# Channel mixing in fp32 on one Trainium2 core: two passes over the tokens, and 2x2 blocks with seven products

## The chip, the cores and the metric

The kernel runs on one core of a Trainium2 chip. The metric is the device time of one execution in microseconds. The engines are named as in the profile: PE (TensorE, matrix multiplication), PEld (its weight loads), DVE (VectorE), ACT (ScalarE), POOL (GpSimd), SP (SyncE, which issues transfers here). SBUF is the on-chip memory, PSUM the accumulators that PE writes, DRAM the memory off the core.

## The reference

All in fp32, batch 8, 8 heads of 64 channels, 576 tokens, 512 channels, 256 token features, 1536 channel features. The four mixing weights come as float64.

```python
kv = np.einsum('bhsd,bhse->bhde', k, v)
out = np.einsum('bhsd,bhde->bhse', q, kv)
rms = np.sqrt(np.mean(out * out, axis=-1, keepdims=True) + 1e-06)
x = out / rms * g_norm                       # then (B, S, H*D) = (8, 576, 512)

h = np.maximum(x.transpose(0, 2, 1) @ w_tok1, 0.0) @ w_tok2
u = x + h.transpose(0, 2, 1)
h2 = np.maximum(u @ w_ch1, 0.0) @ w_ch2      # 512 -> 1536 -> 512 channels
return u + h2
```

## The kernel before

The batches go in four pairs (A, B). A batch has four tiles of 128 tokens and 64 tokens left over; the rests of A and B make one tile, so a pair has 9 tiles, in 3 blocks of 3 for the channel mixing.

`front` (L159) gives the attention and token mixing of a pair as a list of steps: `kv` (L164, k times v, PE line L171, then `load` of the k and v two halves on), `attend` (L203, q times kv, L206) and `attend_rem` (L210, L215) with `norm` (L181: ACT's square L185, DVE's reduction L187, small steps L188 to L199, DVE's multiplication L200 and POOL's multiplication with the gain L201, which gives x), `tok1` (L219, PE L224 and L227, ACT's relu L229), `tok2` (L231, PE L235 and L240, DVE's addition L243, which turns x into u) and `turn_u` (L245: four transposes L250 and an ACT copy L251).

`main` (L265) gives the channel mixing: for each block 12 steps `ch1` (L268: four matmuls of 384 columns, L273, and a relu by ACT L277 or DVE L279 in turn) and 9 steps `ch2` (L281: four matmuls of 512 columns, L287), with DVE's addition of u (L291) and a store.

`decode` (L100) makes fp32 of a piece of weights: POOL's product L112, DVE's clamp L114, shift L116, sign L118, exponent L120 and low word L122, POOL's addition L124. Its raw words are fetched by transfers that ACT issues, into two buffers.

The order of the work is set by `weave` (L308), which deals the steps of one list evenly among those of another; the framework then orders each engine's instructions. The first pair's front is woven with the decodes of the token weights and of `w_ch1`; the first 12 `ch1` with those of `w_ch2`; after that the front of the next pair with the channel mixing of this one:

```python
    for pair in range(B // 2):
        body = main(pair, X, U)
        fill = []
        if pair == 0:
            weave(body[:NF], [do(get_ch2, f) for f in range(NF)])
            body = body[NF:]
        if pair + 1 < B // 2:
            X, U, fill = front(pair + 1)
        weave(body, fill)
```

An fp32 matmul of the program appears in the trace as two matmul records, each with a weight load; a transpose appears as one.

Of the kernel before, what the change touches and what calls it, by code (L numbers as in the profile page):

```python
# [17 lines left out]
def kernel(  # L18
# [35 lines left out]
    NT, NB, TB = 9, 3, 3  # L54
    FG = 4
# [3 lines left out]
    consts = ctx.enter_context(tc.tile_pool(name="consts", bufs=1))  # L59
    inp = ctx.enter_context(tc.tile_pool(name="inp", bufs=2))  # L60
    qtp = ctx.enter_context(tc.tile_pool(name="qtp", bufs=3))
    xp = ctx.enter_context(tc.tile_pool(name="xp", bufs=15))
    work = ctx.enter_context(tc.tile_pool(name="work", bufs=2))
    stage = ctx.enter_context(tc.tile_pool(name="stage", bufs=2))
    mix = ctx.enter_context(tc.tile_pool(name="mix", bufs=3))
    ps_f = ctx.enter_context(tc.tile_pool(name="ps_f", bufs=4, space=bass.MemoryType.PSUM))
    ps_m = ctx.enter_context(tc.tile_pool(name="ps_m", bufs=4, space=bass.MemoryType.PSUM))
# [258 lines left out]
    def do(f, *a):  # L326
        return lambda: f(*a)
# [50 lines left out]
```

## Time and profile before

| | us |
|---|---|
| median of 3 runs | 1053.71 (1050.93 to 1053.9) |
| the profiled execution, span from its first to its last instruction | 1052.2 |
| PE busy | 1002.1 (95%) |
| PEld busy | 537.9 (51%) |
| DVE busy | 266.5 (25%) |
| ACT busy | 100.8 (10%) |
| POOL busy | 106.1 (10%) |

The profile is one execution; its time is given by its span, and the runs' median lies 1.5 us above it. Busy shares are means over stages of different kinds, so they are read by stretches; the chain that ended last goes through PE for 84% of the span, DVE for 9% and transfers for 4%.

### The profile page before, as it was taken

What the parts mean: (1) busy time and instruction counts of PE and PEld (TensorE: products, weight loads), DVE (VectorE), ACT (ScalarE), POOL (GpSimd) and SP (SyncE); (2) the same over time, 40 slices, a digit from 0 to 9 for tenths busy, and PEclk for the clock granted to TensorE, in tenths of its full rate; (3) what the DMA queues carried; (4) which work ended last, traced back from release to release, by engine and by line L of the source; (5) the groups of instructions that cost most, each with busy time, mean ns of one, the idle gap of its engine ahead of it and who ended that gap; (6) DMA issues with size and microseconds to landing.
All of it is one profiled execution on the core that took longest, in us unless ns stands there. A gap on an engine that the chain in (4) does not pass through costs nothing.

```text
span 1052.2 us, 7658 instructions
## 1 busy us (share of the span) xinstructions
PE 1002.1 (95%) x3120; PEld 537.9 (51%) x3120; DVE 266.5 (25%) x559; ACT 100.8 (10%) x214; POOL 106.1 (10%) x100
## 2 busy tenths in 40 slices
PE   4788977999999999999999999999999999999998
PEld 3643544664455466554445456554445445454553
DVE  2898773351011113330111112240011111010000
ACT  0211100020001011111001011011001000000000
POOL 1464441120000001110000000010000000000000
PEclk9789997999999999999999999999999999999999
DMA  8943342121000031300000021000000000000000
GB/s 239 323 147 116 108 142 95 66 90 55 10 11 1 20 100 46 111 10 1 10 21 1 10 65 45 11 20 1 0 21 11 10 21 0 21 10 11 21 0 30
DMA packets 33554, 53.34 MB, mean 51 GB/s; under 512 B 2416, under 2 KB 20848, under 8 KB 33520
## 3 DMA queue, kind: packets, MB, share of 16 engines
q1 hardware_dynamic: 28928, 37.76, 11.0%
q10 hardware_dynamic: 4592, 15.11, 4.6%
q8 instruction: 24, 0.39, 0.2%
q14 instruction: 10, 0.08, 0.0%
HBM read 43.42 MB, written 9.44 MB: 50 GB/s over the span
## 4 chain that ended last, share of the span: by engine, by line
PE 84%; DVE 9%; DMA 4%; POOL 2%; issue 1%; ACTq 0%; ACT 0%; POOLq 0%
PE ps_w L287 35%; PE ps_v L273 33%; PE ps_h L224 4%; PE ps_u L235 4%; PE ps_kv L171 3%; PE ps_o L206 2%; DMA raw<-in_moe_w_tok_dram 2%; DVE part L122 2%; DVE w_ch L118 1%; DVE w_ch L116 1%; DVE w_ch L114 1%; PE ps_h L227 1%; PE ps_ut L250 1%; DVE part L120 1%; POOL w_ch L124 1%; DMA raw<-in_moe_w_ch_dram 1%
## 5 line engine op out<-in xcount | busy, mean ns | idle before, releaser
L287 PE MATMUL ps_w<-w_ch,v 128*128 128x512 f32 x864 | 385.0, 598 | 10.5 <-POOL w_ch L124 10.5
L273 PE MATMUL ps_v<-uT,w_ch 128*128 128x384 f32 x1152 | 383.8, 488 | 1.1 <-DVE v L279 1.1
L273 PEld LDWEIGHTS ps_v<-uT,w_ch 128*128 128x128 f32 x1152 | 215.0, 190 | 151.7 <-issue 13.4
L287 PEld LDWEIGHTS ps_w<-w_ch,v 128*128 128x128 f32 x864 | 161.7, 191 | 208.8 <-issue 190.9
L279 DVE TENSOR_SCALAR v<-ps_v 128x384 f32<-128x384 f32 x72 | 40.0, 556 | 266.2 <-PE ps_v L273 266.2
L201 POOL TENSOR_TENSOR x<-x,g_sb 128x512 f32<-128x512 f32 x36 | 47.8, 1328 | 519.5 <-DVE x L200 517.7
L291 DVE TENSOR_TENSOR o<-ps_w,x 128x512 f32<-128x512 f32 x36 | 24.9, 692 | 259.0 <-PE ps_w L287 258.9
L171 PE MATMUL ps_kv<-v_in,k_in 128*128 128x128 f32 (+1 forms) x320 | 56.0, 323 | 14.9 <-DMA v_in<-in_v_dram 13.8
L277 ACT ACTIVATE v<-ps_v 128x384 f32<-128x384 f32 x72 | 35.3, 490 | 355.2 <-PE ps_v L273 326.4
L235 PE MATMUL ps_u<-h,w_tok 128*128 128x512 f32 x128 | 60.3, 596 | 3.4 <-DVE x L243 3.3
L171 PEld LDWEIGHTS ps_kv<-v_in,k_in 128*128 128x128 f32 (+1 forms) x320 | 48.6, 219 | 27.1 <-issue 20.8
L224 PE MATMUL ps_h<-x,w_tok 128*128 128x512 f32 x128 | 59.7, 610 | 1.7 <-DVE ms L188 1.7
L243 DVE TENSOR_TENSOR x<-ps_u,x 128x512 f32<-128x512 f32 x36 | 24.8, 689 | 96.1 <-PE ps_u L235 78.3
L206 PEld LDWEIGHTS ps_o<-kvp,qT 128*128 128x128 f32 x256 | 37.1, 214 | 16.6 <-issue 4.4
L206 PE MATMUL ps_o<-kvp,qT 128*128 128x128 f32 x256 | 38.6, 302 | 7.1 <-DVE x L200 3.7
L251 ACT COPY uT<-ps_ut 128x512 f32<-128x512 f32 x36 | 21.0, 585 | 219.3 <-PE ps_ut L250 199.8
L187 DVE TENSOR_REDUCE ms<-x 128x8 f32<-128x512 f32 x36 | 24.5, 683 | 67.5 <-ACT x L185 67.5
L224 PEld LDWEIGHTS ps_h<-x,w_tok 128*128 128x128 f32 x128 | 24.7, 195 | 32.1 <-issue 28.9
L235 PEld LDWEIGHTS ps_u<-h,w_tok 128*128 128x128 f32 x128 | 23.8, 190 | 29.8 <-issue 21.1
L124 POOL TENSOR_TENSOR w_ch<-w_ch,part 128x512 f32<-128x512 f32 x24 | 31.4, 1308 | 36.7 <-DVE part L122 34.8
L185 ACT ACTIVATE x<-ps_o 128x512 f32<-128x512 f32 x36 | 21.5, 597 | 90.1 <-PE ps_o L206 75.3
L250 PEld LDWEIGHTS ps_ut<-ident,x 128*128 128x128 f32 x144 | 17.7, 141 | 20.8 <-issue 16.9
(38 smaller groups left out, 281.1 us busy)
## 6 DMA issues: line engine op xcount, KB each, us to landing
raw<-in_moe_w_ch_dram ACTq DMA_DIRECT2D x24, 512.0 KB, 3.6
qT<-in_q_dram SPq DMA_DIRECT2D x8, 1152.0 KB, 5.6
k_in<-in_k_dram SPq DMA_DIRECT2D x16, 512.0 KB, 3.7
v_in<-in_v_dram SPq DMA_DIRECT2D x16, 512.0 KB, 5.5
out_dram<-o SPq DMA_DIRECT2D x32, 256.0 KB, 2.0
raw<-in_moe_w_tok_dram ACTq DMA_DIRECT2D x2, 576.0 KB, 6.1
raw<-in_moe_w_tok_dram ACTq DMA_DIRECT2D x2, 512.0 KB, 9.2
k_in<-in_k_dram SPq DMA_DIRECT2D x16, 64.0 KB, 3.6
```

Of the source, the lines that this page charges most:

```text
L124: nc.gpsimd.tensor_tensor(out=dst, in0=dst, in1=part, op=ALU.add)
L171: nc.tensor.matmul(ps[:, i], lhsT=k_in[r, j, ts(i, P)], rhs=v_in[r, j, ts(i, P)], start=(j == 0), stop=(j == JJ - 1))
L201: nc.gpsimd.tensor_mul(x3, x3, g_sb.to_broadcast([P, H, D]))
L206: nc.tensor.matmul(ps[:, ts(hp, P)], lhsT=qT[side][:, hp, ts(j, P)], rhs=kvp[side][:, hp], start=True, stop=True)
L224: nc.tensor.matmul(ps, lhsT=w_tok1[:, j, ts(t, P)], rhs=X[side * J + j], start=(j == 0), stop=False)
L235: nc.tensor.matmul(ps, lhsT=w_tok2[:, t, ts(i % J, P)], rhs=h1[i // J][:, t], start=(t == 0), stop=(t == NTOK - 1))
L250: nc.tensor.transpose(ps[:, c], X[i][:, ts(c, P)], ident)
L273: nc.tensor.matmul(ps, lhsT=w_ch1[:, c, ts(f, P)], rhs=U[blk][:, c], start=(c == 0), stop=(c == NC - 1))
L277: nc.scalar.activation(dst, ps, AF.Relu)
L279: nc.vector.tensor_scalar(out=dst, in0=ps, scalar1=0.0, scalar2=None, op0=ALU.max)
L287: nc.tensor.matmul(ps, lhsT=v1[i // TB, part][:, f, ts(i % TB, P)], rhs=w_ch2[:, ft], start=(ft == 0), stop=(ft == NF - 1))
L291: nc.vector.tensor_tensor(out=o, in0=ps, in1=X[i], op=ALU.add)
```

## The change

The work is split into two passes. The first does the attention and the token mixing of all four pairs and stores u to nine DRAM tensors of 512 tokens each: eight with the four full tiles of a batch, the ninth with the four tiles of left-over tokens. The second fetches a group of 512 tokens, transposes it and does the channel mixing, one group after the other. The decodes of the channel weights (eight of 768 columns for `w_ch1`, twelve of 512 for `w_ch2`) are dealt among the steps of the first pass.

Both channel products are made as 2x2 blocks: the channels in two halves, the tokens (or outputs) in two halves. Seven products of blocks are made, of sums of blocks on either side, in place of eight. The sums of weights are made once (`mix_ch1`, `mix_ch2`, on POOL), those of the transposed tokens per group (`mix_u`, on DVE), those of the intermediate per round (on DVE and POOL), and the results are put together from PSUM by DVE. A bank of PSUM takes a second product on top of one whose value has been read before.

Smaller edits: `decode` has its first step on ACT and its clamp on POOL; `norm` works on two tiles at a time; k and v have their half tile padded with zeros; the two sides' half-tile matmuls take turns.

```diff
-        nc.gpsimd.tensor_scalar(out=dst, in0=hi.bitcast(F32), scalar1=2.0 ** -112, scalar2=1.0,
-                                op0=ALU.mult, op1=ALU.mult)
-        nc.vector.tensor_scalar(out=dst, in0=dst, scalar1=TOP, scalar2=-TOP,
-                                op0=ALU.min, op1=ALU.max)
+        nc.scalar.activation(dst, hi.bitcast(F32), AF.Copy, scale=2.0 ** -112)
+        nc.gpsimd.tensor_scalar(out=dst, in0=dst, scalar1=TOP, scalar2=-TOP,
+                                op0=ALU.min, op1=ALU.max)
...
+    def mix_ch1():
+        w = [w_ch1[:, i] for i in range(7)]
+        combine(w[4], w[6], w[3], ALU.add)
+        combine(w[5], w[4], w[0], ALU.subtract)
+        combine(w[6], w[0], w[6], ALU.subtract)
+        combine(w[2], w[1], w[5], ALU.subtract)
...
+            if i == 8:
+                nc.sync.dma_start(u_dram[B][ts(pair, P)], x)
+            elif i % 2 == 1:
+                nc.sync.dma_start(
+                    u_dram[2 * pair + i // J][ds((i % J - 1) * P, 2 * P)]
+                    .rearrange("(t p) e -> p t e", p=P), X[pair, i // 2])
...
+    def mix_u(g):
...
+        sub(t1, b[0, 1], b[0, 0])
+        sub(t2, b[1, 1], t1)
+        sub(b[0, 1], b[1, 1], b[0, 1])
+        sub(t4, b[1, 0], t2)
...
+    def channel1(g, d):
...
+        def product(n, ps, start, stop):
+            for w in range(W):
+                for c in range(2):
+                    nc.tensor.matmul(ps[:, w], lhsT=w_ch1[:, n - 1, c, ts(W * d + w, P)],
+                                     rhs=uc[g][n - 1][:, c], start=(start and w == 0 and c == 0),
+                                     stop=stop, skip_group_check=True)
...
+        product(1, p1, True, False)
+        nc.scalar.copy(t1, p1)
+        product(6, p6, True, True)
+        add(u2, p6, t1)
+        product(7, p7, True, False)
+        add(u3, p7, u2)
+        product(5, p5, True, False)
+        add(a22, p5, u3)
+        nc.scalar.activation(a22, a22, AF.Relu)
+        product(2, p1, False, True)
+        nc.scalar.activation(a11, p1, AF.Relu)
+        product(4, p7, False, True)
+        add(a12, p7, u2)
+        nc.scalar.activation(a12, a12, AF.Relu)
+        product(3, p5, False, True)
+        add(s3, p5, u2)
+        nc.vector.scalar_tensor_tensor(out=s1, in0=s3, scalar=0.0, in1=a22,
+                                       op0=ALU.max, op1=ALU.add)
+        nc.vector.scalar_tensor_tensor(out=s3, in0=s3, scalar=0.0, in1=a11,
+                                       op0=ALU.max, op1=ALU.subtract)
+        nc.gpsimd.tensor_tensor(out=s2, in0=s1, in1=a11, op=ALU.subtract)
+        nc.gpsimd.tensor_tensor(out=s4, in0=a12, in1=s2, op=ALU.subtract)
...
+    def channel2(g):
+        def product(n, ps, start, stop):
+            for p in range(2):
+                for s in range(NS):
+                    nc.tensor.matmul(ps[:, p], lhsT=V[g, s // 2][n - 1][:, s % 2, ts(p, P)],
+                                     rhs=w_ch2[:, n - 1, s], start=(start and p == 0 and s == 0),
+                                     stop=stop, skip_group_check=True)
...
+        return [first, sixth, seventh, fifth, second, fourth, third]
...
+    weave(attention(0), weights)
+    weights = [do(get_ch1, i, c) for i in range(2) for c in range(NC)] + [mix_ch1]
+    weights += [do(get_ch2, f) for f in range(NF)] + [mix_ch2]
+    steps = []
+    for pair in range(B // 2 - 1):
+        weave([do(steps.append, f) for f in token_mixing(pair)],
+              [do(steps.append, f) for f in attention(pair + 1)])
+    weave(steps, weights)
...
+    late["m"] = pool("m", 6, space=bass.MemoryType.PSUM)
...
+    for g in range(NG):
+        fetch_u(g + 1)
+        for d in range(NS // 2):
+            channel1(g, d)
+        weave(channel2(g), prepare(g + 1, t_psum))
```

In the diff, `combine` is one POOL addition or subtraction of 1536 columns, `sub` and `add` are one DVE instruction each (`add` reads PSUM), W is 2, NS is 6, and the weights woven with `attention(0)` are the token weights. The functions left out of the diff do what their like did before. In the new program k times v is line L216, attention L251 and L260, the gain multiplication L244, the norm's multiplication L243, the token products L279, L283, L292 and L297, the addition of u L301, the transposes L324, the first channel product L365, the second L404.

How the instructions stand on an engine is shown at three places. On PE, at the end of the first pair's front and the start of its channel mixing before (ps_v and ps_w are the two channel products, ps_ut the transposes, xN is a count of equal matmuls):

```order
L235 MATMUL ps_u<-h_452,w_tok_87 128x512 x2
L250 MATMUL ps_ut<-ident,x 128x128 x4
L240 MATMUL ps_u<-h_427,w_tok_87 64x512 x2
L240 MATMUL ps_u<-h_452,w_tok_87 64x512 x2
L250 MATMUL ps_ut<-ident,x 128x128 x12
L273 MATMUL ps_v<-uT,w_ch_88 128x384 x48
L287 MATMUL ps_w<-w_ch_89,v_662 128x512 x4
L287 MATMUL ps_w<-w_ch_89,v_727 128x512 x4
L171 MATMUL ps_kv<-v_in,k_in 128x128 x10
```

and now, from the last transposes of the second group through its first products (ps_w_1645 takes the last product of the group before, the others are the four banks of a round):

```order
L324 MATMUL ps_ut<-ident,xg 128x128 x4
L404 MATMUL ps_w_1645<-w_ch_89,vs_0_1483 128x256 x2
L404 MATMUL ps_w_1645<-w_ch_89,vs_1_1538 128x256 x2
L404 MATMUL ps_w_1645<-w_ch_89,vs_2_1593 128x256 x2
...
L365 MATMUL ps_v_1786<-uT,w_ch_88 128x256 x4
L365 MATMUL ps_v_1787<-t_1771,w_ch_88 128x256 x4
L365 MATMUL ps_v_1788<-uT,w_ch_88 128x256 x4
L365 MATMUL ps_v_1789<-t_1770,w_ch_88 128x256 x4
L365 MATMUL ps_v_1786<-uT,w_ch_88 128x256 x4
L365 MATMUL ps_v_1788<-t_1772,w_ch_88 128x256 x4
L365 MATMUL ps_v_1789<-uT,w_ch_88 128x256 x4
```

Where runs of 48 and of 4 matmuls of 384 and 512 columns stood, with the next pair's k times v between them, there are now products of 4 (and of 12) matmuls of 256 columns that take turns among PSUM banks, and nothing of the attention. On DVE at the same turn of groups now (there was none before; ps_w_1644 and ps_w_1645 hold the second channel product's last two results, L330 is `mix_u`, L369 and L389 the sums of a round):

```order
L408 TENSOR_TENSOR xg<-ps_w_1644,xg 128x2x256
L330 TENSOR_TENSOR t_1770<-uT 128x512
L330 TENSOR_TENSOR t_1771<-uT,t_1770 128x512
L330 TENSOR_TENSOR uT<-uT 128x2x256
L330 TENSOR_TENSOR t_1772<-uT,t_1771 128x512
L408 TENSOR_TENSOR xg<-ps_w_1645,xg 128x2x256
L369 TENSOR_TENSOR u_1791<-ps_v_1787,t_1790 128x512
```

The four differences of the next group's tokens stand ahead of the last addition of this one. On POOL in the decode of the channel weights before (L201 is the gain multiplication, w_ch_88 is `w_ch1`), the stretch after the first pair's last x:

```order
L201 TENSOR_TENSOR x<-x,g_sb 128x512
L124 TENSOR_TENSOR w_ch_88<-w_ch_88,part 128x512 x2
L112 TENSOR_SCALAR w_ch_88<-raw 128x512 x2
L124 TENSOR_TENSOR w_ch_88<-w_ch_88,part 128x512 x2
L112 TENSOR_SCALAR w_ch_88<-raw 128x512 x2
L124 TENSOR_TENSOR w_ch_88<-w_ch_88,part 128x512
```

and now, from the first pair's last x (the first row) to two of the second pair (w_ch_89 is `w_ch2`, L185 a sum of weights):

```order
L244 TENSOR_TENSOR x<-x,g_sb 128x1024
L134 TENSOR_SCALAR w_ch_88<-w_ch_88 128x768 x2
L144 TENSOR_TENSOR w_ch_88<-w_ch_88,part 128x768 x2
...
L134 TENSOR_SCALAR w_ch_88<-w_ch_88 128x768
L134 TENSOR_SCALAR w_ch_89<-w_ch_89 128x2x256
L244 TENSOR_TENSOR x<-x,g_sb 128x1024
L144 TENSOR_TENSOR w_ch_88<-w_ch_88,part 128x768
L185 TENSOR_TENSOR w_ch_88<-w_ch_88 128x1536 x4
L244 TENSOR_TENSOR x<-x,g_sb 128x1024
L144 TENSOR_TENSOR w_ch_89<-w_ch_89,part 128x2x256
```

The gain multiplications of the second pair, which before came after all decodes, now stand between them and the sums of weights.

## Rows read from the trace of the kernel before

**Rows 1.** The page's slices: busy tenths of PE, and GB/s of the transfers, 40 slices.

```profile
PE   4788977999999999999999999999999999999998
...
GB/s 239 323 147 116 108 142 95 66 90 55 10 11 1 20 100 46 111 10 1 10 21 1 10 65 45 11 20 1 0 21 11 10 21 0 21 10 11 21 0 30
```

**Rows 2.** Windows: stretch, its length, busy us (count) per engine, clock, transfers.

```profile
174.30:861.97 687.67, 687.67 (x2182) 365.85 (x2182) 126.96 (x301) 70.05 (x151) 34.19 (x27) 1.00 0.09 31
861.97:1047.70 185.73, 185.73 (x506) 95.57 (x504) 16.02 (x27) 9.41 (x19) 0.00 (x0) 1.00 0.04 13
```

**Rows 3.** PE in order of time: start, length, line, tile, columns, count.

```profile
861.97 31.13 PE L273 MATMUL ps_v<-uT,w_ch 128*128 128x384 f32 x96
892.93 31.06 PE L287 MATMUL ps_w<-w_ch,v 128*128 128x512 f32 x72
923.83 31.12 PE L273 MATMUL ps_v<-uT,w_ch 128*128 128x384 f32 x96
```

**Rows 4.** Groups of the page: busy us, mean ns of one, idle before and its releaser.

```profile
L273 PEld LDWEIGHTS ps_v<-uT,w_ch 128*128 128x128 f32 x1152 | 215.0, 190 | 151.7 <-issue 13.4
...
L251 ACT COPY uT<-ps_ut 128x512 f32<-128x512 f32 x36 | 21.0, 585 | 219.3 <-PE ps_ut L250 199.8
```

**Rows 5.** PE in order of time, records of 128 columns.

```profile
181.25 1.05 PE L206 MATMUL ps_o<-kvp,qT 128*128 128x128 f32 x8
182.14 3.60 PE L287 MATMUL ps_w<-w_ch,v 128*128 128x512 f32 x8
...
193.34 2.97 PE L171 MATMUL ps_kv<-v_in,k_in 128*128 128x128 f32 x20
196.24 3.70 PE L287 MATMUL ps_w<-w_ch,v 128*128 128x512 f32 x8
```

**Rows 6.** DVE in order of time, from the first pair's last x on.

```profile
68.47 0.68 DVE L200 TENSOR_TENSOR x<-ps_o,inv 128x512 f32<-128x512 f32 x1
...
80.11 1.37 DVE L116 TENSOR_SCALAR w_ch<-w_ch 128x512 uint32<-128x512 uint32 x1
...
85.39 0.43 DVE L114 TENSOR_SCALAR w_ch<-w_ch 128x512 f32<-128x512 f32 x1 [1.99 <-POOL w_ch L112]
85.85 0.43 DVE L116 TENSOR_SCALAR w_ch<-w_ch 128x512 uint32<-128x512 uint32 x1
86.31 0.69 DVE L118 SCALAR_TENSOR_TENSOR w_ch<-raw,w_ch 128x512 uint32<-128x512 uint32 x1
87.03 0.43 DVE L120 TENSOR_SCALAR part<-w_ch 128x512 uint32<-128x512 uint32 x1
87.38 0.68 DVE L243 TENSOR_TENSOR x<-ps_u,x 128x512 f32<-128x512 f32 x1
87.98 0.68 DVE L122 SCALAR_TENSOR_TENSOR part<-raw,part 128x512 f32<-128x512 uint32 x1
...
108.39 0.68 DVE L243 TENSOR_TENSOR x<-ps_u,x 128x512 f32<-128x512 f32 x1
```

**Rows 7.** POOL in order of time, decodes of the channel weights.

```profile
74.55 1.27 POOL L124 TENSOR_TENSOR w_ch<-w_ch,part 128x512 f32<-128x512 f32 x1 [2.28 <-DVE part L122]
...
79.83 1.37 POOL L124 TENSOR_TENSOR w_ch<-w_ch,part 128x512 f32<-128x512 f32 x1 [1.09 <-DVE part L122]
...
92.65 0.65 POOL L112 TENSOR_SCALAR w_ch<-raw 128x512 f32<-128x512 f32 x1 [2.52 <-DMA raw<-in_moe_w_ch_dram]
...
111.88 1.27 POOL L124 TENSOR_TENSOR w_ch<-w_ch,part 128x512 f32<-128x512 f32 x1 [2.28 <-DVE part L122]
```

**Rows 8.** Transfers by line: count, KB each, median us from issue to landing.

```profile
qT<-in_q_dram SPq DMA_DIRECT2D x8, 1152.0 KB, 5.6
```

**Rows 9.** ACT in order of time: its issues of the token weights' transfers.

```profile
22.76 7.61 ACTq L145 DMA_DIRECT2D raw<-in_moe_w_tok_dram  x2
```

**Rows 10.** All engines in order of time, the end of the span.

```profile
1047.75 0.69 DVE L291 TENSOR_TENSOR o<-ps_w,x 128x512 f32<-128x512 f32 x1 [9.61 <-PE ps_w L287]
1048.47 1.11 SPq L299 DMA_DIRECT2D out_dram<-o  x2
```

More of the change, by code (lines that the diff above doesn't have):

```diff
@@ L64, with pool @@
[L64 to L67, printed above, removed]
+    def pool(name, bufs, side="left", stack=ctx, **kw):
+        return stack.enter_context(tc.tile_pool(name=name, bufs=bufs, side=side,
+                                                reuse_waits="tile", **kw))
@@ new lines @@
+    consts = pool("consts", 1)
+    dram = ctx.enter_context(tc.tile_pool(name="dram", bufs=1, space=bass.MemoryType.DRAM))
+    right = ExitStack()
+    xp = pool("xp", 9, "right", right)
+    hp_ = pool("hp", 2, "right", right)
+    left = ExitStack()
+    inp = pool("inp", 1, "left", left)
+    qtp = pool("qtp", 2, "left", left)
+    stage = pool("stage", 2, "left", left)
+    work = pool("work", 2, "left", left)
+    psums = ExitStack()
+    ps_o = pool("ps_o", 2, "left", psums, space=bass.MemoryType.PSUM)
@@ L86, in load, with do, w_psum @@
+    def do(f, *a):
+        return lambda: f(*a)
+    def w_psum(shape, name):
+        return ps_w.tile(shape, F32, name=name, tag="w")
+    qT = {}
     def load(n):
@@ new lines, in norm, with attend @@
+            nc.gpsimd.tensor_mul(x3, x3, g_sb.to_broadcast([P, n * H, D]))
+        def attend(c):
+            side = c // 2
+            ps = ps_o.tile([P, 2, DM], F32, name="ps_o", tag="o")
+            for t in range(2):
+                for hp in range(HP):
+                    nc.tensor.matmul(ps[:, t, ts(hp, P)],
+                                     lhsT=qT[2 * pair + side][:, hp, ts(2 * (c % 2) + t, P)],
+                                     rhs=kvp[side][:, hp], start=True, stop=True)
+            norm(ps, c, 2)
@@ new lines, in attend_rem @@
+        def attend_rem():
+            ps = ps_o.tile([P, 1, DM], F32, name="ps_o", tag="o")
+            for hp in range(HP):
+                for side in range(2):
+                    nc.tensor.matmul(ps[ds(side * HF, HF), 0, ts(hp, P)],
+                                     lhsT=qT[2 * pair + side][:, hp, LO:],
+                                     rhs=kvp[side][:, hp], start=True, stop=True)
+            norm(ps, 4, 1)
+        return [do(kv, 0, 0), do(kv, 0, 1), do(attend, 0), do(kv, 1, 0), do(attend, 1),
+                do(kv, 1, 1), do(attend_rem), do(attend, 2), do(attend, 3)]
@@ L212, in attend_rem, with token_mixing, tok1 @@
+    def token_mixing(pair):
+        h1 = {}
+        def tok1(t):
+            ps = []
+            for side in range(2):
+                if t == 0:
+                    h1[side] = hp_.tile([P, NTOK, DM], F32, name="h1")
+                ps.append(w_psum([P, DM], "ps_h"))
+                for j in range(J):
+                    nc.tensor.matmul(ps[side], lhsT=w_tok1[:, j, ts(t, P)],
+                                     rhs=x_of(pair, side * J + j), start=(j == 0), stop=False)
             for side in range(2):
@@ new lines, in tok2 @@
+            x = x_of(pair, i)
+            nc.vector.tensor_tensor(out=x, in0=ps, in1=x, op=ALU.add)
+            if i == 8:
[4 more added lines that the diff above has]
+                    .rearrange("(t p) e -> p t e", p=P), X[pair, i // 2])
+        return [do(tok1, t) for t in range(NTOK)] + [do(tok2, i) for i in range(9)]
+    xg, uT, uc = {}, {}, {}
```

276 lines of the change are left out of this document (140 added, 136 removed).

## The prediction

> **What bounds the kernel now.** I read the page's slices first, then the stretches by windows, then TensorE's order of time, and last the decode of the weights on VectorE (DVE) and GpSimd (POOL). In the slices TensorE (PE) is below 9 tenths busy only in the first seven [rows 1]. From 174.30 to 1047.70 us it never idles, at a granted clock of 1.00, which is the 2.4 GHz level [rows 2]. So there are two regimes: a start of 174 us in which PE waits for others, and 873 us that are nothing but PE's instructions. A change pays in the second only by taking PE time away, and in the first only by shortening what PE waits for.
>
> The price of a PE instruction is exact in the second regime. Each fp32 matmul of the program is two matmul records. The 96 records of 384 columns of one block run from 861.97 to 892.93, so 30.96/96 = 322.5 ns each, and the 72 of 512 columns that follow run 30.90/72 = 429.2 ns each [rows 3]. The difference is 106.7 ns for 128 columns; what is left beside 0.833 ns a column is 2.5 ns a record. The weight load before each record lasts 190 ns [rows 4] and is hidden at both sizes. At 128 columns eight records of the attention product take 0.89 us (181.25 to 182.14), 111 ns each, but the 20 of k times v 2.90 us (193.34 to 196.24), 145 ns each [rows 5].
>
> **The channel products.** Before: twelve such blocks, 1152 records of 384 and 864 of 512 columns, 371.5 + 370.8 = 742.3 us. After, a group of 512 tokens has three rounds of 7 products with 4 matmuls, and then 7 products with 12: 168 matmuls, all of 256 columns. Nine groups are 1512 matmuls, 3024 records. No row has 256 columns. The line through 384 and 512 gives 322.5 - 106.7 = 215.8 ns; halfway between 111 and 322.5 is 217. From below nothing beats the columns alone, 213 ns; from above the surplus of the k-times-v records over the other 128-column ones (145 - 111 = 34) may be a cost of changing weights quickly, which would make 250. I take 215.8, since two long rows and the eight fast records lie on one line: 3024 x 215.8 = 652.6 us. **That takes away 89.7 us**, by 7/8 of the columns in half as many records again.
>
> The Trainium skill, "TensorE: Matmul & The Clock Gate", section "Back-to-back issue gap", speaks against this change: in a stream of pairs of weight load and matmul both set the spacing, some 81 ns at N=128 where the columns alone give 56. With that surplus of 25 ns the products would take 728 us and all but 14 us of the gain would be gone; the 111 ns rows stand against it, the 145 ns rows for it.
>
> **The sums between products.** In each round DVE adds five products from PSUM (0.68 us each, by the like addition L243) and makes two sums in SBUF (0.69, by the like decode step L118): 4.8 us [rows 6]. ACT makes four passes of about 0.6 [rows 4], POOL two sums of 1.27 [rows 7]. A round is 56 records, 12.1 us of PE, so all of it lies beside PE. The order lets it: a bank that is read after product 1, 7 or 5 is written again two or three products later (1.7 us each), and the four banks of a round rotate over six. Where the second channel product begins, PE has 5.2 us of product 1 and four more matmuls before it needs POOL's last sum, which comes 0.68 + 0.69 + 1.27 = 2.6 us after its input. Where the next group begins, the four differences (4 x 0.7 = 2.8 us) stand on DVE ahead of the last addition, beside the 5.2 us of the last product. I cost these at nothing; if that cover failed, each 0.1 us per product would be 252 x 0.1 = 25 us. The group's read from DRAM is asked for a whole group (74 us) ahead, against 5.6 us for a read of like size [rows 8]. Transposes stay 16 a group: 8 groups x 16 x 0.111 = 14.2 us in this pass.
>
> **The first pass.** It loses its cover. Before, attention and token mixing of pairs 1 to 3 ran between channel matmuls, and what they waited for cost nothing. Now the first pass has only its own PE work: k times v and attention 320 records each at 111, token products 320 at 429, and the first group's transposes: 35.5 + 35.5 + 137.3 + 1.8 = 210 us, 52 a pair. (The padded half tile of k and v removes the 64-row records.)
>
> Beside it stands the decode. In the old trace DVE takes 0.43 + 0.43 + 0.69 + 0.43 + 0.68 = 2.66 us for 512 columns (85.39 to 87.98, five steps [rows 6]) and POOL 0.65 + 1.27 = 1.92, and between POOL's additions of 74.55 and 111.88 lie eight decodes, 4.67 us each: the sum of both and not the longer one [rows 7]. DVE's rows show why: its shift (L116) takes 0.43 us alone, but 1.37 where it starts behind a POOL addition of 1.37, while an addition from PSUM beside a POOL step takes its usual 0.68 [rows 6, 7]. So I add DVE's decode steps to POOL's work, and let its PSUM operations and reductions lie beside POOL.
>
> The Trainium skill, "GPSIMD Engine Reference", section "Key points", draws the same line: POOL shares its SBUF interfaces with DVE instructions in a two-port mode or with two SBUF inputs.
>
> The change gives ACT the first step and POOL the clamp: a decode of 512 is then 2.23 + 1.92 = 4.15, one of 768 is 6.2, and the eight sums of 1536 weights are 3.8 us of POOL each (1.27 per 512). Per pair, POOL's gain multiplication is 9 x 1.27 = 11.4 and DVE's small steps in SBUF some 3.5.
> - To the last x of pair 0: before at 69.2 us [rows 6] with three channel decodes behind it. Now the same three are larger (3 x 1.6) and the five token decodes cheaper (5 x 0.4): 72 us.
> - To the last x of pair 1: five decodes of 768, four of 512, four weight sums, attention: 31 + 16.6 + 15.3 + 14.9 = 78, so 150. PE has 52 there and waits.
> - To the last x of pair 2: eight decodes, four sums, attention: 33.2 + 15.3 + 14.9 = 63, so 213.
> - Then POOL's last multiplication and the rest of the first token product (24 records and the half tiles): 2.5 + 11.5, so 227. From there PE bounds: one pair's 52, then the last second token product and the transposes, 17.2 + 1.8: **pass one ends at 298 us**.
>
> Bounds: if DVE and POOL did not collide, DVE alone has 56 us in the second stage, PE leads from there, and the pass ends near 258. If all of DVE's work added up with POOL's (20 us more in the second stage, 13 in the third), near 331. I take 298 because eight decodes in a row ran at the sum. The intermediate's 9.4 MB out and 9.4 MB back are little beside the 323 GB/s of the second slice [rows 1]. On SP a store of it waits for DVE's addition and holds the k and v loads behind it; they have two buffers and are needed some 9 us later.
>
> **The end.** Before, the last addition starts at 1047.75 and the span ends 4.4 us later, with two stores at 0.55 us of issue each [rows 10]. Now there are four: 5.5 us. I give 2 us to the change of pools between the passes.
>
> **The sum.** 298 + 2 + 652.6 + 14.2 + 5.5 = 972.3 us of span, against 1052.2 now. The shown runs' median, 1053.7, lies 1.5 above that span, so **974 us**, 7.6% less. The products save 89.7; the first pass gives some 10 of it back.
>
> **The rivals.**
> 1. *The first pass is bound by PE, not by DVE and POOL* (it ends at 258): 934 us. For it: POOL also waited up to 2.52 us for its raw data [rows 7], so the 4.67 may hold latency that attention can fill. Against: nine additions were filled in between 87.38 and 108.39 already [rows 6], and the pace stayed.
> 2. *The first pass stretches* (it ends at 331): 1007 us. Everything on DVE and POOL adds up, or the weight DMAs that ACT issues, each waiting for a free raw buffer, hold up ACT's squares and roots. For it: two such issues kept ACT for 7.61 us [rows 9].
> 3. *Weight loads show at 256 columns*, the slower case: 215.8 + 34 = 250 ns a record, 103 us more, 1077 us. It decides from (1053.7 - 974)/3024 = 26.4 ns a record on. For it: the 145 ns records, and a weight load of 190 ns before a record of 213. Against: the eight records at 111, with a load before each; and 4 of the 20 slow ones are 64 rows high, a better reason for their surplus. The page on TensorE named above gives this mechanism 25 ns a record, 1050 us.
> 4. *The change doesn't do what it says*, its columns not falling to 7/8: the order of its instructions, 1512 matmuls of 256 columns, rules it out.
>
> **How the numbers follow.** My forecast 62%, rival 1 15%, rival 2 17%, rival 3 6%. The range from 935 to 1012 holds the forecast, its bounds and nearly all of rivals 1 and 2. Some 0.3% is what a measurement can tell from no change. Rival 3 alone gives slower (5%) or, at three quarters of its price, no change (1%); the rest, 94%, is faster.
>
> **What would show it.** Right: L365 and L404 with 1512 records each, 215 to 217 ns apart; DVE and ACT waiting for PE there, and PE for nothing; a boundary between the passes near 298 us; PE idle between 72 and 227 us, released by the gain multiplication (L244) or DVE's multiplication (L243). Wrong: gaps of PE before products with a releaser on DVE, ACT or POOL; records more than 225 ns apart; a granted clock below 1.00 in the second pass; a boundary before 270 or after 325 us.

## The result, and the profile after

The changed kernel takes 978.3 us (median of four runs) beside 1053.8 for the kernel before in the same comparison: a ratio of 0.930 with a 95% interval from 0.927 to 0.933. The forecast was 974, with a range from 935 to 1012. The profiled execution has a span of 975.2 us.

| | before | after |
|---|---|---|
| span of the profiled execution, us | 1052.2 | 975.2 |
| PE busy, us | 1002.1 | 896.6 |
| PEld busy, us | 537.9 | 723.8 |
| DVE / ACT / POOL busy, us | 266.5 / 100.8 / 106.1 | 383.1 / 148.5 / 246.2 |

The page's slices of the changed kernel, PE's busy tenths and its granted clock (40 slices of 24.4 us), which answer to [rows 1]:

```profile
PE   3749669769999999999999999999999999999997
...
PEclk9879879889999999999999999999999999999999
```

PE is below nine tenths in seven of the first nine slices, then in none but the last. The windows of the stages (stretch, length, then busy us and count of PE, PEld, DVE, ACT and POOL, clock, share and GB/s of the transfers); the cuts are the ends of the four first token products, the first channel product and PE's last record:

```profile
12.12:84.51 72.39, 47.51 (x200) 31.50 (x200) 50.83 (x77) 15.28 (x25) 34.92 (x24) 0.83 0.76 238
84.51:159.70 75.19, 57.61 (x242) 33.57 (x241) 60.12 (x84) 15.87 (x28) 44.84 (x27) 0.86 0.56 186
159.70:231.95 72.25, 55.81 (x243) 33.68 (x241) 49.39 (x73) 12.23 (x23) 37.19 (x21) 0.91 0.52 167
231.95:302.23 70.28, 68.68 (x299) 38.09 (x297) 30.95 (x60) 12.52 (x24) 10.68 (x5) 1.00 0.39 135
302.23:969.20 666.97, 666.97 (x3154) 586.97 (x3152) 189.04 (x276) 89.96 (x149) 115.70 (x81) 1.00 0.07 25
969.20:975.20 6.00, 0.03 (x1) 0.00 (x0) 0.69 (x1) 0.00 (x0) 0.00 (x0) 0.95 0.38 89
```

Two regimes again. From 302.23 to 969.20 us PE is busy for all of 666.97 us; before that, it waits for 73 of 302. PE in order of time, at the start of the first second channel product (the answer to [rows 3]):

```profile
338.59 5.34 PE L404 MATMUL ps_w<-w_ch,v 128*128 128x256 f32 x24
343.77 5.34 PE L404 MATMUL ps_w<-w_ch,vs 128*128 128x256 f32 x24
348.95 0.60 PE L324 MATMUL ps_ut<-ident,xg 128*128 128x128 f32 x4
```

24 records take 5.18 us twice, 215.8 ns each. The groups of the second pass (busy us, mean ns; idle before) show what waits there:

```profile
L365 PE MATMUL ps_v<-uT,w_ch 128*128 128x256 f32 x864 | 201.3, 379 | 0.0
...
L365 PEld LDWEIGHTS ps_v<-uT,w_ch 128*128 128x128 f32 x864 | 164.1, 190 | 23.1 <-issue 0.8
```

PE waits for nothing there, and the weight load of 190 ns is hidden beside a record of 215.8. (The 379 ns are a record's own length, with a modelled end; what counts is the distance from one start to the next.) In the first pass DVE and POOL, in order of time, behind pair 1's first x (in brackets the idle time before and its releaser):

```profile
112.08 14.18 POOL L185 TENSOR_TENSOR w_ch<-w_ch 128x1536 f32<-128x1536 f32 x4
```

```profile
86.95 0.56 DVE L136 TENSOR_SCALAR w_ch<-w_ch 128x768 uint32<-128x768 uint32 x1 [6.40 <-POOL w_ch L134]
...
104.16 0.16 DVE L240 SCALAR_TENSOR_TENSOR root<-root,ms 128x16 f32<-128x16 f32 x1
...
112.21 1.21 DVE L230 TENSOR_REDUCE ms<-x 128x16 f32<-128x1024 f32 x1
113.34 0.68 DVE L301 TENSOR_TENSOR x<-ps_u,x 128x512 f32<-128x512 f32 x1
...
116.39 3.11 DVE L238 SCALAR_TENSOR_TENSOR ms<-ms,inv 128x16 f32<-128x16 f32 x1
...
119.63 3.27 DVE L240 SCALAR_TENSOR_TENSOR root<-root,ms 128x16 f32<-128x16 f32 x1
```

Four sums of weights hold POOL for 14.18 us, 3.5 each. While they run, a reduction and an addition from PSUM take their usual 1.21 and 0.68 us. Two steps of 16 columns, whose like takes 0.16 at 104.16, take 3.11 and 3.27, until 119.50 and 122.90, just behind the ends of the second and the third sum (112.08 + 2 x 3.55 and + 3 x 3.55). But at 86.95 DVE has idled for 6.40 us with the decode on its way. The waits of the same pass (total us, times, longest) say what for; below them ACT in order of time, ahead of that step.

```profile
DVE w_ch L136 <- POOL w_ch L134: 31.2, 11, 6.4
ACT w_ch L133 <- DMA raw<-in_moe_w_ch_dram: 30.2, 11, 6.3
```

```profile
84.61 0.60 ACT L286 ACTIVATE h<-ps_h 128x512 f32<-128x512 f32 x1 [6.66 <-PE ps_h L283]
85.11 0.90 ACT L133 ACTIVATE w_ch<-raw 128x768 f32<-128x768 f32 x1
```

So two things stretch the first pass: the collision of POOL's long instructions with DVE's (theory A, the forecast's), and a round trip of the decode, raw transfer to ACT to POOL to DVE, with two raw buffers (theory B). The longest wait, at 86.95, is neither alone: ACT has the decode's first step (L133) behind a relu that waited 6.66 us for PE. No run moves that step alone. The experiments separate theories A and B as far as they can, and test the second pass.

### The profile page after: what moved, and what is told of

Read it like the earlier page. It is cut to its first block, busy times and chain, and to the rows that moved or that the text cites. A ratio compares the mean times of both kernels' runs of the same rounds, so it can differ in the third digit from the quotient of the medians.

```text
span 975.2 us, 10020 instructions
## 1 busy us (share of the span) xinstructions
PE 896.6 (92%) x4128; PEld 723.8 (74%) x4128; DVE 383.1 (39%) x573; ACT 148.5 (15%) x252; POOL 246.2 (25%) x169
## 4 chain that ended last, share of the span: by engine, by line
PE 78%; DVE 11%; DMA 4%; POOL 4%; issue 1%; ACT 1%; SPq 0%; ACTq 0%; DVEq 0%; POOLq 0%
PE ps_v L365 33%; PE ps_w L404 33%; PE ps_u L292 3%; DMA raw<-in_moe_w_ch_dram 3%; PE ps_h L279 3%; PE ps_kv L216 2%; DVE part L142 2%; PE ps_ut L324 2%; POOL w_ch L185 1%; POOL x L244 1%; DVE x L243 1%; PE ps_o L251 1%; DVE w_ch L138 1%; DVE part L140 1%; DVE ms L230 1%
## 5 line engine op out<-in xcount | busy, mean ns | idle before, releaser
L365 PE MATMUL ps_v<-uT,w_ch 128*128 128x256 f32 x864 | 201.3, 379 | 0.0
L404 PE MATMUL ps_w<-w_ch,vs 128*128 128x256 f32 x864 | 192.1, 379 | 0.0
L365 PEld LDWEIGHTS ps_v<-uT,w_ch 128*128 128x128 f32 x864 | 164.1, 190 | 23.1 <-issue 0.8
L404 PEld LDWEIGHTS ps_w<-w_ch,vs 128*128 128x128 f32 x864 | 162.3, 190 | 21.1
L393 POOL TENSOR_TENSOR vs<-vs,v 128x512 f32<-128x512 f32 x27 | 47.6, 1764 | 428.3 <-DVE vs L389 410.4
L365 PE MATMUL ps_v<-t,w_ch 128*128 128x256 f32 x648 | 153.1, 379 | 0.0
L404 PE MATMUL ps_w<-w_ch,v 128*128 128x256 f32 x648 | 144.1, 379 | 0.0
L365 PEld LDWEIGHTS ps_v<-t,w_ch 128*128 128x128 f32 x648 | 123.1, 190 | 16.7
L404 PEld LDWEIGHTS ps_w<-w_ch,v 128*128 128x128 f32 x648 | 122.5, 190 | 16.3
L279 PE MATMUL ps_h<-x,w_tok 128*128 128x512 f32 x128 | 65.5, 654 | 16.4 <-POOL x L244 16.4
L369 DVE TENSOR_TENSOR v<-ps_v,u 128x512 f32<-128x512 f32 x54 | 37.3, 692 | 102.1 <-PE ps_v L365 102.1
L251 PE MATMUL ps_o<-kvp,qT 128*128 128x128 f32 x256 | 40.2, 319 | 30.4 <-DVE x L243 17.7
L251 PEld LDWEIGHTS ps_o<-kvp,qT 128*128 128x128 f32 x256 | 37.7, 228 | 40.5 <-issue 23.0
L279 PEld LDWEIGHTS ps_h<-x,w_tok 128*128 128x128 f32 x128 | 25.0, 208 | 52.9 <-issue 29.0
L292 PE MATMUL ps_u<-h,w_tok 128*128 128x512 f32 x128 | 61.8, 614 | 1.4 <-ACT h L286 1.4
L244 POOL TENSOR_TENSOR x<-x,g_sb 128x1024 f32<-128x1024 f32 (+1 forms) x20 | 44.2, 2210 | 61.4 <-DVE x L243 58.6
L216 PEld LDWEIGHTS ps_kv<-v_in,k_in 128*128 128x128 f32 x320 | 41.0, 206 | 20.8 <-issue 19.5
L216 PE MATMUL ps_kv<-v_in,k_in 128*128 128x128 f32 x320 | 42.1, 291 | 13.9 <-DMA v_in<-in_v_dram 13.9
```

The source lines that it names most:

```text
L216: nc.tensor.matmul(ps[:, i], lhsT=kk[:, j, ts(i, P)], rhs=vv[:, j, ts(i, P)], start=(j == 0), stop=(j == JJ - 1))
L244: nc.gpsimd.tensor_mul(x3, x3, g_sb.to_broadcast([P, n * H, D]))
L251: nc.tensor.matmul(ps[:, t, ts(hp, P)], lhsT=qT[2 * pair + side][:, hp, ts(2 * (c % 2) + t, P)], rhs=kvp[side][:, hp], start=True, stop=True)
L279: nc.tensor.matmul(ps[side], lhsT=w_tok1[:, j, ts(t, P)], rhs=x_of(pair, side * J + j), start=(j == 0), stop=False)
L292: nc.tensor.matmul(ps, lhsT=w_tok2[:, t, ts(i % J, P)], rhs=h1[i // J][:, t], start=(t == 0), stop=(t == NTOK - 1))
L365: nc.tensor.matmul(ps[:, w], lhsT=w_ch1[:, n - 1, c, ts(W * d + w, P)], rhs=uc[g][n - 1][:, c], start=(start and w == 0 and c == 0), stop= ...
```

## The experiments

All times are medians; ratios are to the kernel before, measured beside it. The stages, read from the one profiled execution of each kernel: the end of the first token product of pairs 0 to 3 and the start of the first channel product, us.

| kernel | time | ratio, 95% interval | pair 0 | pair 1 | pair 2 | pair 3 | second pass |
|---|---|---|---|---|---|---|---|
| the change | 978.3 | 0.927 to 0.933 | 84.6 | 159.8 | 232.0 | 284.7 | 302.2 |
| e1_eight | 1053.7 | 0.9996 to 1.0022 | 85.5 | 152.4 | 215.1 | 267.9 | 286.3 |
| e2_no_wsum | 964.8 | 0.914 to 0.918 | 89.8 | 156.7 | 220.8 | 273.5 | 291.0 |
| e3_raw5 | 970.4 | 0.919 to 0.924 | 90.9 | 164.2 | 225.0 | 277.8 | 295.3 |
| e4_dve | 959.8 | 0.909 to 0.913 | 82.0 | 149.2 | 214.9 | 267.7 | 285.2 |
| s1_sums_twice | 982.0 | 0.929 to 0.934 | 86.7 | 161.6 | 236.4 | 289.1 | 306.6 |
| f2_late_dve | 949.5 | 0.899 to 0.902 | 82.0 | 143.3 | 203.6 | 256.4 | 273.9 |
| f3_late_dec | 972.6 | 0.921 to 0.926 | 86.2 | 152.1 | 204.8 | 256.8 | 290.1 |
| f4_late_dec_dve | 957.1 | 0.905 to 0.910 | 81.0 | 143.1 | 195.9 | 247.8 | 280.0 |
| g1_late_raw5 | 953.1 | 0.903 to 0.906 | 85.3 | 146.2 | 206.9 | 259.7 | 277.3 |
| g2_late_sp | 961.3 | 0.911 to 0.914 | 81.7 | 143.6 | 196.4 | 249.1 | 282.0 |
| h1_spread | 940.6 | 0.891 to 0.895 | 82.5 | 133.7 | 190.1 | 244.2 | 261.9 |

**The two passes alone.**

```diff
+    def channel1(g, f):
+        v = V[g, f] = late["v"].tile([P, DM], F32, name=f"v{f}")
+        ps = m_psum([P, DM], "ps_v")
+        for c in range(NC):
+            nc.tensor.matmul(ps, lhsT=w_ch1[:, c, ts(f, P)], rhs=uT[g][:, c],
+                             start=(c == 0), stop=(c == NC - 1))
...
+        def tile_of(t):
+            ps = m_psum([P, DM], "ps_w")
+            for f in range(NF):
+                nc.tensor.matmul(ps, lhsT=V[g, f][:, ts(t, P)], rhs=w_ch2[:, f],
+                                 start=(f == 0), stop=(f == NF - 1))
```

> The two passes alone: the second pass makes eight products of 512 columns in place of seven of 256, and no sums of weights, tokens or results are made. The second pass has 9 x 192 x 2 = 3456 records of 429.2 ns, some less at its transposes: 742 from the first to the last product's records of 512 x 2 x 864 (1728 matmuls, 3456 records at 214.6 ns per 256 columns) + 14 = 756 us against the 667 measured with the scheme. The first pass also loses its eight sums of weights. If POOL's and DVE's work add up in the first pass (theory A), it ends near 275 instead of 302 and the span is about 275 + 756 + 6 = 1037 us. If the decode's round trip and its raw buffers set the pace (theory B), the sums lie beside waiting, the pass ends near 295 and the span is about 1057. Either way the scheme is worth about 90 us in the second pass; if the sums or weight loads had cost PE anything there, it would be less.

It takes what the kernel before takes, within the 0.3% that can be told. Its first pass ends at 286.3, halfway between theory A's 275 and theory B's 295. Its window of the second pass, beside the change's 666.97 (PE's 1856 records are 1728 of 512 columns and 128 transposes; the 3456 of the expectation count 256 columns each):

```profile
286.26:1046.63 760.37, 758.02 (x1856) 341.27 (x1856) 61.59 (x89) 51.07 (x86) 0.00 (x0) 1.00 0.06 21
```

So the scheme takes 93.4 us from the second pass, and the first pass is 15.9 longer with it (302.2 against 286.3); the tail is 1.3 longer. The net, 76.2, is the 76.1 between the spans (1051.3 and 975.2). Dividing the work into passes, with the smaller edits, gains nothing and costs nothing by itself.

**The sums of weights left out.**

```diff
-    weights += [do(get_ch2, f) for f in range(NF)] + [mix_ch2]
+    weights += [do(get_ch2, f) for f in range(NF)]
```

(`mix_ch1` likewise. DVE fills the empty slots with zeros at the start of the kernel, from 2.53 to 11.57 us.)

> The sums of weights are left out (their slots hold zeros, so three of seven products of each kind are wrong; PE's work is the same). Eight POOL instructions of 3.5 us go. Theory A (POOL's work and DVE's decode steps add up): pass one ends near 275 us, the time is about 951. Theory B (round trip of the decode, raw buffers): at most 8 us less, about 970. The second pass stays at 667 us.

11.2 us less in the first pass: neither 27 nor 8 at most. The second and third stage are 67 and 64 us in place of 75 and 72. Each lost 14 us of POOL and gave back 8. The first stage is 5.2 us longer, with the zeros ahead of the decode on DVE; without that the sums are worth some 16 us, like the 15.9 of e1_eight, which has none either, and half of the 30.6 that the forecast charged. Either POOL's work and DVE's do not add up in full, or another wait takes the place of the sums; this run does not tell which. Nor do the busy times of the windows, since DVE's 60.12 us in the second stage hold the time in which it stood behind POOL.

**Five raw buffers.**

```diff
     def fetch(n):
+        i = turn[0] = (turn[0] + 1) % 5
+        if i < 3:
+            spare = w_ch2[:, 3 + i].rearrange("p s n -> p (s n)").bitcast(U32)
+            return spare[:, :2 * n].rearrange("p (n w) -> p n w", w=2)
         return stage.tile([P, n, 2], U32, name="raw", tag="raw")
```

> Five raw buffers instead of two, three of them in slots of w_ch2 that are not written before its sums. Theory A: no change within 5 us (978). Theory B: the stops behind raw transfers go; four of them in the chain of waits between 91 and 190 us last 7.07, 6.02, 4.28 and 5.79 us, 23 together, so the time falls to about 955. If the issues from ACT stood in ACT's way, they no longer wait for a buffer, and that gain is in the same number.

The third stage falls from 72.3 to 60.8 us, the second from 75.2 to 73.3, and the first grows by 6.3, since more channel decodes come ahead of the first pair's x: eight of the large ones are done by its end in place of five. The stages' gains are thus in part work moved forward, and the net is what counts: 6.9 us of the first pass, 7.9 of the median. Theory B is real, and a third of the 23 us that it forecast.

**All of the decode's POOL work on DVE.**

```diff
-        nc.gpsimd.tensor_scalar(out=dst, in0=dst, scalar1=TOP, scalar2=-TOP,
+        nc.vector.tensor_scalar(out=dst, in0=dst, scalar1=TOP, scalar2=-TOP,
...
-        nc.gpsimd.tensor_tensor(out=dst, in0=dst, in1=part, op=ALU.add)
+        nc.vector.tensor_tensor(out=dst, in0=dst, in1=part, op=ALU.add)
...
-        nc.gpsimd.tensor_tensor(out=o, in0=a, in1=b, op=op)
+        nc.vector.tensor_tensor(out=o, in0=a, in1=b, op=op)
```

> The clamp, the last addition and the sums of weights move from POOL to DVE; POOL keeps the gain multiplication alone. Theory A: the collisions go. DVE has about 24 units of 512 columns x 3.34 = 80 us of channel decode, 17 of token decode, 16 of weight sums and 20 a pair of its own, 193 us in all by 227, so PE leads more often: pass one ends at 260 to 270 and the time is about 940. Theory B: the round trip loses two crossings between engines but waits for raw data as before: 5 to 10 us less, about 970. Rival: DVE becomes the bound itself and the first pass is longer than 302 us.

17 us gained in the first pass, more than from five buffers or from leaving the sums out, though DVE was given all that work. 959.8 lies between theory A's 940 and theory B's 970 and decides for neither. DVE is then near to being the bound: it is busy for 58.3 of 67.2 us in the second stage and 54.9 of 65.7 in the third. The window from 120 to 160 us:

```profile
120.00:160.00 40.00, 29.34 (x110) 15.45 (x109) 35.62 (x60) 7.60 (x14) 8.05 (x3) 0.91 0.46 149
```

Here DVE (the third pair of numbers) is busy for 35.62 of 40 us and PE (the first) for 29.34.

**DVE's additions in the second pass made twice.**

```diff
+            nc.vector.tensor_tensor(out=tmp(shape, "spare"), in0=ps, in1=x, op=ALU.add)
             nc.vector.tensor_tensor(out=o, in0=ps, in1=x, op=ALU.add)
```

> In the second pass each of DVE's additions from PSUM is made twice, the first time into a spare tile: 9 groups x (3 x 5 + 6) = 189 more of about 0.65 us, 123 us of DVE in 667, and every sum is ready 0.65 us later than before. If the sums lie beside the products with room, as I costed them, the time stays at 978 within 3 us: DVE goes from about 28% to 46% of the second pass and the results of a product are wanted only after the next one (1.73 us). Rival: the chain of sums stands at the edge already; then 0.65 us for each of the 189 shows in part, 30 to 120 us more.

```profile
306.56:973.50 666.94, 666.94 (x3154) 587.37 (x3152) 303.69 (x464) 86.90 (x149) 115.98 (x81) 1.00 0.07 25
```

The second pass is the same to 0.03 us with DVE at 303.69 us instead of 189.04, so the 3.7 us more in the whole come from the first pass (306.6 against 302.2). Every engine has the same instructions in the same order there; some 4 us is thus what the first pass of one order of work can differ by between two kernels, and nothing is built on less below.

**The sums behind pair 3's last x, and the decode on DVE.**

```diff
+            last[:] = [square, nc.vector.tensor_mul(x3, o, inv.to_broadcast([P, n * H, D])),
+                       nc.gpsimd.tensor_mul(x3, x3, g_sb.to_broadcast([P, n * H, D]))]
...
+            with tc.issue_after(last[0].ins), tc.issue_after(last[1].ins), tc.issue_after(last[2].ins):
+                f(*a)
...
-    weave(token_mixing(3), prepare(0, lambda: w_psum([P, NC, P], "ps_ut")))
+    weave(token_mixing(3), mix_ch1() + mix_ch2() + prepare(0, lambda: w_psum([P, NC, P], "ps_ut")))
```

(`issue_after` keeps an engine's order; `mix_ch1` and `mix_ch2` now return lists of single sums, each of them run through the middle lines.)

> The eight sums of weights stay on POOL but are queued behind pair 3's last gain multiplication, where POOL was busy for 11 of 70 us; the decode's clamp and last addition move to DVE, so that POOL has the gain multiplication alone beside DVE's decode. Theory A (what POOL and DVE do in SBUF adds up): the run with everything on DVE ended its first pass at 285 us with DVE busy for some nine tenths of the time up to 200 us; 14 us of weight sums leave DVE, so 272 us, time about 946. Theory B (raw transfers set the pace): no more than 4 us off that run, about 956.

949.5: 3 us from theory A, 7 from B. With the 4 us above this favours A and does not settle it. POOL's sums cost nothing where DVE has little but additions from PSUM: from pair 3's first token product to the second pass it is 17.5 us with them and without.

**Eight late decodes as well.**

```diff
-    weights += [do(get_ch2, f) for f in range(NF)] + [mix_ch2]
+    weights += [do(get_ch2, f) for f in range(4)]
...
+    weave(token_mixing(3), mix_ch1() + [behind(get_ch2, f) for f in range(4, NF)] + mix_ch2() +
+          prepare(0, lambda: w_psum([P, NC, P], "ps_ut")))
```

> Engines of the decode as in the changed kernel. The eight sums of weights and the decodes of the last eight of twelve pieces of w_ch2, raw transfers included, are queued behind pair 3's last x, under the 70 us in which PE is busy throughout; stages two and three keep eight decodes of 768 columns and four of 512. Theory A: 16 units of 4.15 instead of 24, and no sums: 33 + 15 = 48 us for either stage, less than PE's 52, so each stage takes 55 to 58 us instead of 75 and 72, and the pass ends near 270: about 945. Theory B: the first eight pieces come at the same pace as before, and the second stage stays near 66 us as without sums; the third falls to 55: the pass ends near 278, about 953. Danger: the late decodes take 63 us beside PE's 70, and the first products wait for them.

> Both together: late sums on POOL, eight late decodes, clamp and last addition of every decode on DVE. Theory A: DVE has 16 x 3.34 = 53 us of decode in stages two and three together and about 20 a stage of its own, 47 a stage, under PE's 52: the pass ends near 265, about 940; as good as or a little better than with the decode's engines unchanged. Theory B: the same as that run within 4 us.

972.6 and 957.1 miss both theories of either kernel. The third stage falls to PE's own 52.8 us in both, as forecast. The last stage gives it back: 33 and 32 us from pair 3's first token product to the second pass instead of 17.5. The second of the two kernels in order of time, first POOL, then DVE, ACT and PE:

```profile
238.24 14.31 POOL L185 TENSOR_TENSOR w_ch<-w_ch 128x1536 f32<-128x1536 f32 x4
```

```profile
242.07 7.21 DVE L136 TENSOR_SCALAR w_ch<-w_ch 128x512 uint32<-128x512 uint32 x2
249.20 4.50 DVE L138 SCALAR_TENSOR_TENSOR w_ch<-raw,w_ch 128x512 uint32<-128x512 uint32 x2
```

```profile
255.05 0.33 ACTq L180 DMA_DIRECT2D raw<-in_moe_w_ch_dram  x1
255.43 0.60 ACT L290 ACTIVATE h<-ps_h 128x512 f32<-128x512 f32 x1 [15.75 <-issue]
```

```profile
261.77 12.92 PE L296 MATMUL ps_u<-h,w_tok 128*128 128x512 f32 x26 [12.92 <-ACT h L290]
```

PE's wait points at ACT's relu, the relu stands behind an issue of a raw transfer, and the issue waited for a raw buffer which DVE held through two steps of 3.6 us that take 0.43 alone. Which link matters, the issue on ACT or the collision, the next run decides.

**ACT taken out of the late decodes; five buffers with the decode on DVE.**

```diff
-        nc.scalar.dma_start(raw, words(moe_w_ch2)[ts(f, P)])
+        (nc.sync if late else nc.scalar).dma_start(raw, words(moe_w_ch2)[ts(f, P)])
...
+        if late:
+            nc.gpsimd.tensor_scalar(out=dst, in0=hi.bitcast(F32), scalar1=2.0 ** -112,
+                                    scalar2=1.0, op0=ALU.mult, op1=ALU.mult)
```

> The run with late sums, eight late decodes and the decode on DVE, in which PE stood still for 12.92 us before the second token product of pair 3: ACT had an issue of a raw transfer ahead of its relu, and that issue waited for a raw buffer. Here the eight late pieces are fetched by SP and their first step is POOL's; ACT has nothing of them. If the issue on ACT is the cause, the 12.9 us go and the time is about 944. If the collision of POOL's sums of weights with DVE's decode is the cause, PE waits for DVE (the addition of u) instead and the time stays near 957.

PE's wait stays, at 12.0 us, now for DVE's addition of u (L311), which stands behind the decode steps. POOL (L190 is a sum of weights), DVE and PE in order of time:

```profile
242.76 10.56 POOL L190 TENSOR_TENSOR w_ch<-w_ch 128x1536 f32<-128x1536 f32 x3
```

```profile
242.84 3.64 DVE L139 TENSOR_SCALAR w_ch<-w_ch 128x512 f32<-128x512 f32 x1 [6.52 <-POOL w_ch L135]
246.51 3.53 DVE L141 TENSOR_SCALAR w_ch<-w_ch 128x512 uint32<-128x512 uint32 x1
250.08 3.79 DVE L143 SCALAR_TENSOR_TENSOR w_ch<-raw,w_ch 128x512 uint32<-128x512 uint32 x1
```

```profile
268.16 7.51 PE L302 MATMUL ps_u<-h,w_tok 128*128 128x512 f32 x12 [11.96 <-DVE x L311]
```

So the issue on ACT is not the cause; it only passed the wait on. Each of the three steps lasts as long as one sum of weights, 3.5 us, instead of 0.43 or 0.69: that is 9.4 us, and 6.52 more go by before them, while POOL has the decode's first step between two sums. What is not parted here is how long PE would wait for an addition of u behind late decodes that collide with nothing. 961.3 is 4 us worse than with ACT, which is not read as a difference.

> The run with late sums and the decode on DVE, and beside it five raw buffers instead of two (three in slots of w_ch2 that its sums write later). If waits for raw data still cost what five buffers gave back when POOL and DVE both decoded (8 us), the time falls from 949.5 to about 942. If they only show beside collisions, it stays at 949.5 within 2 us: DVE, busy for some nine tenths of the second and third stage, is then what bounds them.

No gain; the 3.6 us more are the first stage's 3.3. The second and third stage are 60.9 and 60.7 us against 61.3 and 60.3, so raw buffers no longer hold them. That DVE does is not shown: in f2_late_dve it is busy for 52.8 and 47.0 us of these two stages, less than the nine tenths that I had put down, and PE for 54.0 and 53.4.

**All on DVE, dealt by stage.**

```diff
+    weights[7:] = [behind(1, weights[7])] + [behind(1, get_ch2, f) for f in range(6)]
...
+    weave(token_mixing(3), mix_ch1() + [behind(3, get_ch2, f, True) for f in range(6, NF)] +
+          mix_ch2() + prepare(0, lambda: w_psum([P, NC, P], "ps_ut")))
```

(With the edits of e4_dve and g2_late_sp; `behind(p, ...)` queues behind pair p's last x.)

> All of the decode and the sums of weights on DVE, so that POOL has nothing with two SBUF inputs but the gain multiplication, and the work dealt by stage: seven pieces of w_ch1 up to pair 1's last x, the eighth and six of w_ch2 behind it, the other six pieces (fetched by SP, first step on POOL) and the eight sums behind pair 3's last x. If the collision of POOL's long additions with DVE was what made the late decodes cost what they gave, DVE has about 25 + 25 us a stage in stages two and three (under PE's 52) and 58 of the last 70: stages of 55 to 58, 53 and 53 us, pass one ends at 262 to 268, the time is about 938. If it is the late decodes as such (DVE's additions of u queued behind them), PE waits for DVE in the last stage again and the time is 950 or more.

940.6 us, 0.893 of the kernel before and 38 us better than the change. Stages two to four take 51.2, 56.4 and 54.1 us, PE's own being 52, and the second pass begins at 261.9. PE does not wait in the last stage. Against g2_late_sp two things changed at once, no sums on POOL and six late decodes instead of eight; what each gave is not shown. This is the best version found. PE still idles for 42 us before that (261.9 less 219.9 busy), 12.5 of them for the first transfer; taking these away was not tried.

## Why the prediction was right, and where it was not

**The channel products.** Right to the digit: 215.8 ns a record measured, as the line through 384 and 512 columns gave, and 666.97 us for the second pass beside 652.6 + 14.2. The upper end of 250 ns had its reason in the k-times-v records of 145; PE in order of time now, with no record of 64 rows among them, has

```profile
88.56 2.40 PE L216 MATMUL ps_kv<-v_in,k_in 128*128 128x128 f32 x20
90.80 1.88 PE L292 MATMUL ps_u<-h,w_tok 128*128 128x512 f32 x4
```

so 20 of them from 88.56 to 90.80, 112 ns each: the surplus was the rows', as the third rival's "against" had it. The page "TensorE: Matmul & The Clock Gate" of the Trainium skill, section "Back-to-back issue gap", has 25 ns more for a weight load and a matmul at 128 columns; no run here shows that, neither at 128 nor at 256 fp32 columns, and the measurement decides.

**The sums between products.** Right: no wait of PE in the second pass, and none with DVE's additions doubled.

**The first pass.** 302.2 measured, 298 predicted. The milestone of the prediction, DVE's last multiplication of a pair, is the end of these rows:

```profile
67.52 1.22 DVE L243 TENSOR_TENSOR x<-ps_o,inv 128x1024 f32<-128x1024 f32 x1
...
145.66 1.23 DVE L243 TENSOR_TENSOR x<-ps_o,inv 128x1024 f32<-128x1024 f32 x1
...
218.02 1.23 DVE L243 TENSOR_TENSOR x<-ps_o,inv 128x1024 f32<-128x1024 f32 x1
```

That is 68.7 for pair 0 (72 predicted), 146.9 for pair 1 (150) and 219.3 for pair 2 (213); the end of pair 2's first token product is 232.0 (227). From one to the next it took 78.2 (78), 72.4 (63), 12.8 (14) and, to the end of the pass, 70.2 (71). The one stretch off by more than 5 us is the third, with "63", and half of its 9 us was made up by the others, 3.3 of it before pair 0's x.

What was missing in the third is the wait for raw data. The chain that ended last goes through these raw transfers, the first in the second stretch, the others in the third:

```profile
91.09 7.07 DMA raw<-in_moe_w_ch_dram
...
154.46 3.60 DMA raw<-in_moe_w_ch_dram
...
166.44 6.02 DMA raw<-in_moe_w_ch_dram
...
177.71 4.28 DMA raw<-in_moe_w_ch_dram
...
184.73 5.79 DMA raw<-in_moe_w_ch_dram
```

These are 7.1 and 19.7 us, for which I had no term. The rule behind the terms, DVE's decode steps added to POOL's work, was only partly right. Its direction holds (the collision is shown in the rows, in f4_late_dec_dve and in g2_late_sp), but the "15.3" for four sums of weights gave back 8 when they were left out. So the second stretch came out right by luck: a term that charged some 7 us too much stood beside a wait of 7.1 that had no term. In the third the waits were longer, and the sum was off. How much they cost by themselves is not shown; five buffers gained 6.9 us of the whole pass.

**The clock.** I counted PE's own work in the first pass at 210 us; the windows' busy times there add up to 229.6, at a granted clock of 0.83 to 0.91 in the three stages in which PE waits. PE in order of time shows four equal records early and after two longer waits (of 6.38 us, ahead of the group before, and 3.91):

```profile
39.30 1.98 PE L279 MATMUL ps_h<-x,w_tok 128*128 128x512 f32 x4 [0.90 <-POOL x L244]
...
71.84 3.78 PE L279 MATMUL ps_h<-x,w_tok 128*128 128x512 f32 x4 [3.91 <-POOL x L244]
```

The first four ran at a granted clock of 1.00, the second at 0.50, the lower of the two levels (1.2 GHz), and take nearly twice as long. In h1_spread, with PE kept busier, the first pass has 219.9 us of PE at a mean clock of 0.95. The last stage, where PE sets the end, ran at 1.00. Ahead of it the chain that ended last goes through slow records twice, these four and 16 of the attention (3.76 us at 134.14, at 0.50, beside 1.95 at 103.09), so the clock may have put up to 3.6 us into the milestones, for which I had no term. In the other direction, the 210 us had the second token product of the left-over tokens too dear:

```profile
300.36 1.94 PE L297 MATMUL ps_u<-h,w_tok 128*64 128x512 f32 x8
302.23 1.99 PE L365 MATMUL ps_v<-uT,w_ch 128*128 128x256 f32 x8
```

Eight of its records take 1.87 us, 234 ns each and not 429, as they did in the kernel before (103.97 to 105.84).

**The end.** 6.0 us from PE's last record where I had 5.5. The 2 us for the change of pools did not show: the first channel product follows without a wait.

**The rivals.** The first (the pass ends at 258) did not happen, but its bound is real: h1_spread reaches 261.9 by placing the same work elsewhere. The second (331) did not; its mechanism, an issue on ACT that holds up what stands behind it, shows in f4_late_dec_dve, as a consequence of the collision; in the change itself it cost PE a wait of 1.35 us at 167.50, behind a relu that stood behind such an issue. The third fell with the 215.8 ns.

## What to carry to other kernels

A saving on the engine that bounds a regime is worth its full price if the others keep room there: seven products for eight took 93 us of PE, and the sums that they need vanished beside it. Their one-off preparation fell where PE was already waiting; such work belongs in the stretch where PE is the bound, and long additions of POOL do not belong beside DVE's steps in SBUF. Where a wait names an engine (ACT's relu), follow it to the instruction that is itself late before moving anything.

## What the runs showed that was not expected

A DVE step from SBUF to SBUF that meets a running POOL addition waits for its end whatever its own size: 0.16 us for 16 columns became 3.27, and 0.43 for 512 columns 3.6, beside sums of 3.5 us. Reductions and additions from PSUM went on at 1.21 and 0.68, and reciprocals of 16 columns at 0.24 and 0.25 (116.12 and 122.93). The Trainium skill, "SBUF — State Buffer", section "Who interferes with whom", says this: the ports that VectorE and GpSimd share are locked for a whole instruction, the loser stands still, and reductions are exempt. These rows agree. Five raw buffers helped only while POOL shared the decode (970.4 after 978.3, but 953.1 after 949.5).
